# Grouping the bf16 products, pairing the state updates and placing the opening's zero products in an mLSTM plus gated-MLP kernel

## The chip, the cores and the metric

The kernel runs on one core of one Trainium2 chip. A core has five instruction engines: TensorE (PE in the profile, with its weight loads listed as PEld), VectorE (DVE), ScalarE (ACT), GpSimd (POOL) and SyncE (SP), which here issues all DMA transfers. The metric is the device time in microseconds of one execution; several executions of the same kernel are run and their median is given.

## The reference

The first half is a recurrent attention (mLSTM) for 4 batches, 8 heads, 768 steps and head size 40. For each step, with gates f and i in log space and a running maximum m:

```python
m_new = max(f[t] + m, i[t])
C = exp(f[t] + m - m_new) * C + exp(i[t] - m_new) * outer(v[t], k[t])
n = exp(f[t] + m - m_new) * n + exp(i[t] - m_new) * k[t]
y[t] = sigmoid(o_gate[t]) * (C @ q[t]) / max(abs(n @ q[t]), 1)
```

The second half takes y as 3072 tokens of 320 features and computes `((x @ w_a) * (x @ w_b)) @ w_out`, with 1536 hidden features. All inputs and outputs are float32; the weights arrive as float64 bit patterns and are converted on the chip.

## The kernel before

**Attention in chunks.** The 768 steps of each batch are cut into 6 chunks of 128 steps, so there are 24 chunks (chunk n is time piece c = n // 4 of batch b = n % 4). Within a chunk the recurrence is a masked product: pS holds the products of k and q per head, gbc the exponentials of the gates (also the product of both, which becomes the left operand), pV the product with v (42 columns for a head: 40 of v, one of ones for the normalizer, one pad), pI the contribution of the state carried in from earlier chunks, and pU the update of that state, k times the weighted v (vw), 8 heads of 42 columns each. The state of a batch lives in the tile cst; two heads share its 128 partitions, so every pU matmul has 64 output partitions. pX is the transpose of the finished chunk (osig) into the tiles xh and xl, from which the second half starts.

**Precision.** From chunk 6 on (NF32 = 6) the attention works in bf16 pieces: each float32 operand is split into a high, a middle and a low bf16 part. For pV a head then takes 6 matmuls of 42 columns (pb, gbc's middle part and again pb against va, vr, vl), 48 for a chunk; for pS two matmuls of 128 columns a head, 16 for a chunk in two halves of 4 heads; for pI 16 matmuls of 42 columns. The first chunks use plain float32 products instead, which take two passes on PE. The state used by the bf16 chunks is split in the same way (cb, cr), written to DRAM (c_dram) and read back in another layout (cx).

**The gated MLP in blocks.** Tokens go through the MLP in 9 blocks of 2 or 3 chunks (256 or 384 columns). Each of the 12 hidden pieces (ff) has two accumulators pu (for w_a and w_b), 8 matmuls each in float32r with the operands split in high and low parts (xh, xl and the two halves of w), then the product g, its split gh, gl, and 3 matmuls of 320 columns for each chunk into pd.

**Weights.** 32 stages of weights are loaded as raw, converted by ACT and DVE to cw and then to the pair of float32r halves in the tile w (the high half by a cast, the low half by a DVE subtraction).

**What sets the order.** The program is written as Python generators that interleave one attention chunk with the MLP block before it, but no instruction is issued at once. Everything is recorded in a Plan: consecutive matmuls are put together in a node (Plan.add), which is issued as a whole; Plan.cost gives each node an estimated cost; Plan.run goes through time and, for each engine, takes from the ready nodes the one with the smallest rank; Plan.settle repeats this with varied ranks (TURNS turns) and tries each order on TRIALS varied sets of costs; Plan.emit then issues the best order, engine by engine. Some small operations may go to either of two engines (copier: ACT or DVE; adder: DVE or POOL), and the plan chooses. A node of PE holds up to 8 matmuls that write the same accumulator, or (with plan.pair set) different ones. In the opening, while PE has little to do, the plan issues filler matmuls of zeros (warm, 256 columns, line 515 of the profile); ten larger ones (512 columns) come first. Nearly all instructions are issued from line 522, so the profile is read by tile names rather than by lines.

**Buffers and loads near the change.** q and k of chunk n share the tile qk[n % 3], v is in va[n % 3]. The loads of chunk n + 2 are recorded at the start of chunk n (aside, letter L). vr and vl, the lower parts of v, have two buffers each, vw one, cb one. pU is written to the PSUM ring of the attention (pat, two banks) from chunk 6 on.

The functions that the change touches are:

## Time and profile before

| what | value |
|---|---|
| median of 3 runs | 534.64 us (534.57 to 535.79) |
| the profiled execution | 534.12 us |
| its span, first to last instruction | 532.3 us |
| PE busy | 523.2 us, 98% of the span |
| PE weight loads busy | 497.1 us |
| DVE busy | 411.4 us, 77% |
| ACT busy | 236.3 us, 44% |
| POOL busy | 147.9 us, 28% |
| mean granted TensorE clock | 0.994 |

The profile gives start times in microseconds from the first instruction of the span. A matmul's listed duration runs until its result is complete, and matmuls overlap, so what a matmul costs PE is the step from its start to the start of the next one, not its listed duration. A weight load (PEld) overlaps the matmul before it. Where a row covers several matmuls (x2, x16), its time is that of all of them. In a group view the columns after the bar are the total busy time, the mean of one in ns, and the idle time of the engine before these instructions with what ended it.

### The profile page before, as it was taken

What the parts mean: (1) busy time and instruction counts of PE and PEld (TensorE: products, weight loads), DVE (VectorE), ACT (ScalarE), POOL (GpSimd) and SP (SyncE); (2) the same over time, 40 slices, a digit from 0 to 9 for tenths busy, and PEclk for the clock granted to TensorE, in tenths of its full rate; (3) what the DMA queues carried; (4) which work ended last, traced back from release to release, by engine and by line L of the source; (5) the groups of instructions that cost most, each with busy time, mean ns of one, the idle gap of its engine ahead of it and who ended that gap; (6) DMA issues with size and microseconds to landing.
All of it is one profiled execution on the core that took longest, in us unless ns stands there. A gap on an engine that the chain in (4) does not pass through costs nothing.

```text
span 532.3 us, 12505 instructions
## 1 busy us (share of the span) xinstructions
PE 523.2 (98%) x4862; PEld 497.1 (93%) x4862; DVE 411.4 (77%) x919; ACT 236.3 (44%) x568; POOL 147.9 (28%) x194
## 2 busy tenths in 40 slices
PE   8889999999999999999999999999999999999997
PEld 6679999999999999999999999999999999999997
DVE  5999999799979859888599776888489848843332
ACT  5759997543456142346243344543215515212111
POOL 2015134414326505534223423526050301000000
PEclk9899999999999999999999999999999999999999
DMA  9998866978696864886755766765537427000001
GB/s 172 305 245 182 238 167 135 137 148 165 117 188 129 148 146 104 155 158 104 169 105 97 158 119 157 155 99 114 130 73 140 93 41 156 2 1 25 2 1 37
DMA packets 198679, 66.77 MB, mean 125 GB/s; under 512 B 184252, under 2 KB 191900, under 8 KB 198620
## 3 DMA queue, kind: packets, MB, share of 16 engines
q1 hardware_dynamic: 198620, 65.98, 59.6%
q8 instruction: 38, 0.62, 0.5%
q14 instruction: 21, 0.17, 0.1%
HBM read 41.11 MB, written 5.97 MB: 88 GB/s over the span
## 4 chain that ended last, share of the span: by engine, by line
PE 81%; DVE 7%; issue 3%; DMA 2%; ACT 2%; SPq 1%; POOL 0%; ACTq 0%; DVEq 0%; POOLq 0%
PE pu L522 46%; PE pd L522 22%; PE pV L522 4%; PE pS L522 3%; PE pU L522 2%; DVE qks L522 2%; DVE w L522 2%; PE pI L522 2%; SPq L522 1%; PE pX L522 1%; DMA qk<-in_k_dram 1%; DVE cw L522 1%; DMA gbc<-g_dram 1%; DMA c_dram<-cb 1%; DVE osig L522 1%
## 5 line engine op out<-in xcount | busy, mean ns | idle before, releaser
L522 PE MATMUL pu<-xh,w 128*128 128x384 f32 (+1 forms) x1080 | 277.2, 325 | 0.1
L522 PE MATMUL pu<-xl,w 128*128 128x384 f32 (+1 forms) x648 | 203.9, 323 | 0.9 <-DVE xl L522 0.9
L522 PEld LDWEIGHTS pu<-xh,w 128*128 128x128 f32 x1080 | 190.0, 189 | 1.7 <-ACT xh L522 0.6
L522 PE MATMUL pd<-w,gh 128*128 128x320 f32 x576 | 135.1, 315 | 0.3 <-ACT gh L522 0.2
L522 PEld LDWEIGHTS pu<-xl,w 128*128 128x128 f32 x648 | 121.1, 189 | 1.4 <-DVE xl L522 1.2
L522 PEld LDWEIGHTS pd<-w,gh 128*128 128x128 f32 x576 | 97.0, 188 | 1.0 <-ACT gh L522 0.7
L522 DVE TENSOR_TENSOR g<-pu,g 128x384 f32<-128x384 f32 (+1 forms) x108 | 54.6, 506 | 53.4 <-PE pu L522 50.2
L522 ACT COPY g<-pu 128x384 f32<-128x384 f32 (+1 forms) x99 | 43.7, 442 | 113.8 <-PE pu L522 112.6
L522 PE MATMUL pd<-w,gl 128*128 128x320 f32 x288 | 86.6, 310 | 0.1
L522 ACT ACTIVATE gbc<-gbc,gtab 128x128 f32<-128x128 f32 x160 | 52.7, 394 | 3.3 <-POOL gbc L522 3.3
L522 PEld LDWEIGHTS pd<-w,gl 128*128 128x128 f32 x288 | 53.4, 188 | 0.3 <-DVE gl L522 0.3
L522 POOL TENSOR_TENSOR gl<-g,gh 128x384 fp32r<-128x384 f32 (+1 forms) x24 | 26.4, 1102 | 81.4 <-ACT gh L522 46.0
L522 DVE TENSOR_TENSOR gl<-g,gh 128x384 fp32r<-128x384 f32 (+1 forms) x84 | 46.4, 553 | 2.1 <-DVE gh L522 0.5
L522 ACT CAST gh<-g 128x384 fp32r<-128x384 f32 (+1 forms) x44 | 20.5, 465 | 39.9 <-DVE g L522 39.8
L522 DVE TENSOR_TENSOR gbc<-pS,gbc 128x512 f32<-128x512 f32 x48 | 32.6, 681 | 4.7 <-ACT gbc L522 3.7
L522 POOL TENSOR_TENSOR vr<-va 128x336 f32<-128x336 f32 x18 | 14.0, 775 | 79.0 <-PE pV L522 71.1
L522 PE MATMUL pV<-va,gbc 128*128 128x42 bf16 (+1 forms) x240 | 34.5, 221 | 0.0
L522 POOL TENSOR_TENSOR vw<-va,gtab 128x336 f32<-128x336 f32 x20 | 16.2, 808 | 64.9 <-PE pU L522 58.1
L522 PEld LDWEIGHTS <-T 120*128 120x128 bf16 x576 | 25.4, 97 | 7.6 <-issue 5.1
L522 DVE TENSOR_TENSOR gbc<-gbc,pb 128x512 f32<-128x512 f32 x36 | 29.4, 817 | 0.4 <-ACT pb L522 0.3
L522 DVE TENSOR_TENSOR pb<-gbc 128x512 bf16<-128x512 f32 x36 | 29.0, 806 | 0.3
L522 POOL TENSOR_SCALAR_AFFINE_SELECT gbc<-gbc 128x1024 f32<-128x1024 f32 x20 | 25.0, 1248 | 11.7 <-DMA gbc<-g_dram 11.7
(109 smaller groups left out, 768.7 us busy)
## 6 DMA issues: line engine op xcount, KB each, us to landing
gbc<-g_dram SPq DMA_DIRECT2D x20, 512.0 KB
qk<-in_q_dram SPq DMA_DIRECT2D x24, 160.0 KB
qk<-in_k_dram SPq DMA_DIRECT2D x24, 160.0 KB
va<-in_v_dram SPq DMA_DIRECT2D x24, 160.0 KB
osig<-in_o_gate_dram SPq DMA_DIRECT2D x24, 160.0 KB
raw<-in_moe_w_out_dram SPq DMA_DIRECT2D x12, 320.0 KB
out_dram<-o SPq DMA_DIRECT2D x24, 160.0 KB
raw<-in_moe_w_a_dram SPq DMA_DIRECT2D x8, 384.0 KB
```

Of the source, the lines that this page charges most:

```text
L522: f(*[real(x) for x in args], **{k: real(x) for k, x in kw.items()})
```

## The change

The change has these parts:

- **Groups.** A PE node may hold 24 matmuls instead of 8 when the stationary operand of the recorded matmul is a bf16 tile, and 16 when plan.pair is set. The 48 matmuls of pV become two nodes of 24 (one for each half of the heads) instead of six of 8, the 16 of pI one node instead of two; the two nodes of pS stay at 8.
- **Order on PE.** Each PE node has now a head (what its first weight load costs), a tail (its last matmul) and a mode (64 rows, 64 columns or full). When a node with a long head would follow a short matmul, Plan.run looks for another ready node with a short head whose rank is not more than BAND = 15 behind and takes that first. The difference of head and tail, and 0.085 us for a change of mode, are added to the planned time. The assumed cost of a float32r matmul changes too.
- **Search.** TURNS goes from 40 to 100, and the varied costs on which orders are tried are spread less.
- **Two chunks' state at once.** The states of two batches lie in one tile (cst2). stage_u does nothing for even n; for odd n it records 16 pU matmuls, 8 for chunk n - 1 and 8 for chunk n, into one accumulator of 336 columns, then one update of both states on DVE (or one copy on ACT) and one split (cb, cr) of double width. The subtractions of the split may now go to DVE or POOL, and the middle cast to ACT or DVE. put_state and get_state are called for both chunks, so the state of an even chunk is written one chunk later.
- **Loads and buffers.** Since pU of chunk n - 1 reads its k only after chunk n, for odd n >= 3 the load of k of chunk n + 2 (which goes to the same tile) is recorded at the end of stage_u(n), q and v stay where they were. vw has two buffers instead of one, vr and vl one instead of two.
- **Zero products.** The fillers of the opening are placed by what PE has done in the last 3.4 us: they fill a known gap while that use is under 80% (FULL), and up to four are put ahead of a node where it is under 42% (LEAST, FORCED).

```diff
 PSUM = bass.MemoryType.PSUM
-TURNS = 40
+TURNS = 100
 TRIALS = 4
...
 SPELL = 3.4133
+BAND = 15.0
+GAP = 0.1
+FULL = 0.8
+LEAST = 0.42
+FORCED = 4
...
 class Node:
-    __slots__ = ("i", "eng", "alts", "calls", "by", "prev", "next", "table", "acc", "wide", "use", "pair", "least")
+    __slots__ = ("i", "eng", "alts", "calls", "by", "prev", "next", "table", "acc", "wide", "use", "pair", "least", "head", "tail", "mode")
...
         self.table, self.wide, self.use = None, True, 0.0
+        self.head, self.tail, self.mode = None, 0.0, 0
...
         if not (
-            alts[0] == "PE" and node is not None and node.eng == "PE" and len(node.calls) < 8
+            alts[0] == "PE" and node is not None and node.eng == "PE" and len(node.calls) < (24 if getattr(refs[1], "size", 4) == 2 else 16 if self.pair else 8)
             and (node.acc[0][0] == okey or self.pair and node.pair)
...
                 elif "float32r" in f32[0]:
-                    occ = cols / 2400 + 0.0135
+                    occ = cols * 0.000452 + 0.0015
                 else:
...
             by[1] = 0.17
+            node.mode = 1 if refs[1].shape[0] <= 64 else 2 if out.shape[0] <= 64 else 0
+            node.tail = occ
+            if node.head is None:
+                node.head = (0.03 if size[1] == 2 else 0.107) / (2 if node.mode == 2 else 1)
             plain = size[1] == 4 and op == "matmul" and "float32r" not in f32[0]
...
         other = {"DVE": "POOL", "POOL": "DVE"}
-        order, count, filling = [], 0, False
+        order, count, filling, mode, tail, recent = [], 0, False, 0, 1.0, []
...
                     found = i
+            if e == "PE" and found is not None and tail < 0.06 and nodes[found].head > tail + 0.04:
+                like = [
+                    (k, i) for k, i in ready[e]
+                    if not done[i] and k < rank[found] + BAND and nodes[i].head < tail + 0.04
+                ]
+                if like:
+                    back.append((rank[found], found))
+                    found = min(like)[1]
+                    ready[e].remove((rank[found], found))
+                    heapq.heapify(ready[e])
             for z in back:
...
                     filling = False
-                z = free[e] + 0.2
+                z, forced = free[e], 0
                 while filling and fixed is None:
                     w = int((z + phase) / SPELL)
-                    z += 0.107 if used.get(w - 1, 0.0) >= 0.375 * SPELL * 2400 else 0.214
-                    if z > t:
+                    span = 0.107 if used.get(w - 1, 0.0) >= 0.375 * SPELL * 2400 else 0.214
+                    lately = sum(u for at_, u in recent if at_ > z - SPELL)
+                    if z + span < t - GAP and lately < FULL * SPELL * 2400:
+                        pass
+                    elif z > 3.0 and lately < LEAST * SPELL * 2400 and forced < FORCED:
+                        forced += 1
+                    else:
                         break
+                    recent.append((z, 256))
                     used[w] = used.get(w, 0.0) + 256
+                    z += span
                     order.append(None)
+                t = max(t, z)
+                recent.append((t, x.use))
+                del recent[:-60]
+                t += max(0.0, x.head - tail)
+                if x.mode != mode:
+                    t += 0.085
+                    mode = x.mode
+                tail = x.tail
                 w = int((t + phase) / SPELL)
...
         odds = [
-            (rng.uniform(0.98, 1.07, n), 1.0 + 0.025 * j, 0.1 * j, SPELL * j / TRIALS)
+            (rng.uniform(1.0 - 0.005 * j, 1.0 + 0.012 * j, n), 1.0 + 0.01 * j, 0.06 * j, SPELL * j / TRIALS)
             for j in range(TRIALS)
...
-    cst = [wpool.tile([P, HH, DV], F32, name=f"cst{b}") for b in range(B)]
+    cst2 = [wpool.tile([P, 2 * HH, DV], F32, name=f"cst{b}") for b in range(B // 2)]
+    cst = [cst2[b // 2][:, b % 2 * HH:(b % 2 + 1) * HH] for b in range(B)]
     cxp = [[wpool.tile([P, H, DV], BF16, name=f"cx{b}_{w}") for w in range(2)] for b in range(B)]
...
         x = nat(n)[1]
-        vr = apool.tile([P, H, DV], F32, tag="vr", name=f"vr{n}")
-        vl = apool.tile([P, H, DV], BF16, tag="vl", name=f"vl{n}")
+        vr = apool.tile([P, H, DV], F32, tag="vr", name=f"vr{n}", bufs=1)
+        vl = apool.tile([P, H, DV], BF16, tag="vl", name=f"vl{n}", bufs=1)
         s["vb"] = (top(x), top(vr), vl)
...
         if c < NC - 1:
-            vw = apool.tile([P, H, DV], F32, tag="vw", name=f"vw{n}", bufs=1)
+            vw = apool.tile([P, H, DV], F32, tag="vw", name=f"vw{n}", bufs=2)
             nc.gpsimd.tensor_tensor(
...
     def stage_u(n):
+
         c, b = chunks[n]
-        if c == NC - 1:
+        if c == NC - 1 or n % 2 == 0:
             return
-        s = st[n]
         if n < 6:
...
             pU = ps_at.tile([P, 512], F32, tag="pat", name=f"pU{n}")
-        pu = pU[:, 0:HH * DV].rearrange("p (h d) -> p h d", h=HH)
-        for h in range(H):
-            r, _, x = half(h)
-            nc.tensor.matmul(
-                pu[r:r + 64, x], nat(n)[0][:, 1, h, :], s["vw"][:, h], start=True, stop=True
-            )
-        t = cst[b]
+        pu = pU[:, 0:H * DV].rearrange("p (h d) -> p h d", h=H)
+        plan.pair = True
+        for j, m in enumerate((n - 1, n)):
+            for h in range(H):
+                r, _, x = half(h)
+                nc.tensor.matmul(
+                    pu[r:r + 64, j * HH + x], nat(m)[0][:, 1, h, :], st[m]["vw"][:, h],
+                    start=True, stop=True,
+                )
+        plan.pair = False
+        t = cst2[b // 2]
         if c == 0:
...
             nc.vector.tensor_tensor(
-                t, t, dec[:, c - 1, b * HH:(b + 1) * HH].unsqueeze(2).broadcast_to([P, HH, DV]),
+                t, t, dec[:, c - 1, (b - 1) * HH:(b + 1) * HH].unsqueeze(2).broadcast_to([P, H, DV]),
                 op=ALU.mult,
...
         yield
-        if n + B < NF32:
-            return
-        cb = apool.tile([P, 3, HH, DV], BF16, tag="cb", name=f"cb{n}", bufs=1)
-        cr = apool.tile([P, H * DV], F32, tag="tmp", name=f"cr{n}")[:, 0:HH * DV]
-        cr = cr.rearrange("t (h d) -> t h d", h=HH)
-        nc.scalar.copy(cb[:, 2], t)
-        nc.gpsimd.tensor_tensor(cr, t, cb[:, 2], op=ALU.subtract)
-        yield
-        if n < 8:
-            nc.scalar.copy(cb[:, 1], cr)
-        else:
-            nc.vector.tensor_copy(cb[:, 1], cr)
-        nc.gpsimd.tensor_tensor(cb[:, 0], cr, cb[:, 1], op=ALU.subtract)
-        states[n] = cb
-        yield
+        if n + B >= NF32:
+            cb = apool.tile([P, 3, H, DV], BF16, tag="cb", name=f"cb{n}", bufs=1)
+            cr = apool.tile([P, H * DV], F32, tag="tmp", name=f"cr{n}")
+            cr = cr.rearrange("t (h d) -> t h d", h=H)
+            nc.scalar.copy(cb[:, 2], t)
+            nc.adder.tensor_tensor(cr, t, cb[:, 2], op=ALU.subtract)
+            yield
+            nc.copier.copy(cb[:, 1], cr)
+            nc.adder.tensor_tensor(cb[:, 0], cr, cb[:, 1], op=ALU.subtract)
+            states[n - 1], states[n] = cb[:, :, 0:HH], cb[:, :, HH:]
+            yield
+        if n > NS and n + 2 < NCH:
+            load_qk(n + 2, (1,))
...
     def stage_d(n):
-        s = st[n] if n < NS else st.pop(n)
+        s = st[n]
         k_ = block[n]
...
         if o == "L" and n + 2 < NCH and n + 2 > NS + 1:
-            load(n + 2)
+            whole = n % 2 == 0 or chunks[n][0] == NC - 1
+            load_qk(n + 2, (0, 1) if whole else (0,))
+            load_v(n + 2)
         if o == "P":
+            put_state(n - 2)
             put_state(n - 1)
...
         if o == "C":
+            get_state(n - 2)
             get_state(n - 1)
...
         c, b = chunks[n]
-        vw = apool.tile([P, H, DV], F32, tag="vw", name=f"vw{n}", bufs=1)
+        vw = apool.tile([P, H, DV], F32, tag="vw", name=f"vw{n}", bufs=2)
         nc.gpsimd.tensor_tensor(
...
-    idle = apool.tile([P, H * DV], F32, tag="vr", name="idle").bitcast(BF16)[:, 0:512]
+    idle = apool.tile([P, H * DV], F32, tag="vr", name="idle", bufs=1).bitcast(BF16)[:, 0:512]
     nc.vector.memset(idle, 0.0)
...
             if n == 0:
-                load(NS + 1)
+                load_qk(NS + 1, (0,))
+                load_v(NS + 1)
+            else:
+                load_qk(NS + 1, (1,))
         squash(0, NS, B - NS)
...
         yield from attention()
```

The written-out orders of the two programs are compared at three places. The first is on PE, at the state update of chunk 13. In these rows pV13 is the accumulator of chunk 13, pU13 the state update, vw12 and vw13 the weighted v of chunks 12 and 13, and gbc13, pb13, va1, vr13 operands of pV. Before:

```order
L522 MATMUL pV13_4174<-va1_84,gbc13_3624 128x42
L522 MATMUL pU13_4191<-vw13_3910,qk1_81 64x42 x8
L522 LDWEIGHTS gbc13_3624
L522 MATMUL pV13_4174<-vr13_3613,gbc13_3624 128x42
L522 LDWEIGHTS pb13_0_3965
```

The change:

```order
L557 MATMUL pV13_4060<-vr13_3848,gbc13_3479 128x42
L557 LDWEIGHTS pb13_0_3864
L557 MATMUL pV13_4060<-va1_84,pb13_0_3864 128x42
L557 MATMUL pU13_4087<-vw12_3489,qk0_80 64x42 x8
L557 MATMUL pU13_4087<-vw13_3547,qk1_81 64x42 x8
L557 MATMUL pd3_0_3373<-w30_1334,gh3_10_4018 128x320 x2
L557 MATMUL pd3_0_3373<-w30_1334,gl3_10_4023 128x320
```

The update of chunk 12 has moved from its own place to directly ahead of that of chunk 13. In the whole program pU comes in 20 separate places before and in 10 now.

The second place is on PE at the start of chunk 15, whose first product is pS15_0; pu4 and pd4 are accumulators of MLP block 4, T15 the transposed q and k. Before, the two nodes of pS15 stand apart, between float32r matmuls:

```order
L522 MATMUL pS15_0_4594<-T15_0_4406,T15_1_4444 128x128
L522 MATMUL pu4_5_1_4570<-xl4_3485,w12_716 128x384
L522 MATMUL pd4_1_4359<-w13_821,gh4_3_4463 128x320
L522 MATMUL pd4_0_4331<-w13_821,gh4_3_4463 128x320 x2
L522 MATMUL pd4_0_4331<-w13_821,gl4_3_4467 128x320
L522 MATMUL pd4_1_4359<-w13_821,gh4_3_4463 128x320
```

The change:

```order
L557 LDWEIGHTS gbc14_3860
L557 MATMUL pV14_4440<-vr14_4205,gbc14_3860 128x42
L557 LDWEIGHTS pb14_1_4343
L557 MATMUL pV14_4440<-va2_85,pb14_1_4343 128x42
L557 LDWEIGHTS T15_1_4286
L557 MATMUL pS15_0_4491<-T15_0_4318,T15_1_4286 128x128
```

pS15_0 now follows the last of the 48 matmuls of pV14 with no float32r matmul between. Counted over the whole PE order, a bf16 run of the attention is followed by a matmul into pu or pd 99 times before and 44 times now.

The third place is on DVE in the opening, right after the first gates (qks2_88, cx3). pS0 and gbc0 belong to chunk 0, T1 is the transposed q or k of chunk 1, cw, raw0, qks0 and w0 are the first stage of weights. Before:

```order
L522 COPY cx3_1_101<-qks2_88 32x256
L522 TENSOR_TENSOR gbc0_231<-pS0_0_221,gbc0_231 128x4x128
L522 COPY T1_251<-pT1_1_246 128x512
L522 TENSOR_TENSOR gbc0_231<-pS0_1_223,gbc0_231 128x4x128
L522 TENSOR_SCALAR cw_289<-raw0_176 128x384
L522 SCALAR_TENSOR_TENSOR cw_289<-qks0_86,cw_289 128x384
```

The change:

```order
L557 COPY cx3_1_99<-qks2_88 32x256
L557 TENSOR_SCALAR cw_239<-raw0_164 128x384
L557 COPY T1_252<-pT1_0_231 128x512
L557 SCALAR_TENSOR_TENSOR cw_239<-qks0_86,cw_239 128x384
L557 TENSOR_TENSOR gbc0_225<-pS0_0_241,gbc0_225 128x4x128
L557 TENSOR_TENSOR gbc0_225<-pS0_1_243,gbc0_225 128x4x128
```

A copy of T1 and the first two steps of the first weight now stand ahead of the product of pS0 with gbc0. The opening's 256-column zero products are 52 before and 65 now.

## The prediction

> **What bounds the kernel now.** I read the page first (the span and the busy shares), then the busy times by windows, then who PE waits for after the opening.
>
> ```profile
> span 532.3 us, 12505 instructions
> PE 523.2 (98%) x4862; PEld 497.1 (93%) x4862; DVE 411.4 (77%) x919; ACT 236.3 (44%) x568; POOL 147.9 (28%) x194
> ```
>
> ```profile
> core 0: us, PE busy (x) PEld busy (x) DVE busy (x) ACT busy (x) POOL busy (x), PEclk, DMA share, GB/s
> 45.00:80.00 35.00, 34.80 (x324) 33.09 (x322) 33.98 (x82) 34.48 (x84) 10.27 (x14) 1.00 0.75 190
> 100.00:460.00 360.00, 359.55 (x3513) 344.49 (x3512) 295.26 (x643) 147.30 (x366) 118.35 (x135) 1.00 0.64 127
> ```
>
> ```profile
> PE pu L522 <- DVE xl L522: 0.9, 1, 0.9
> PE pE L522 <- ACT gbc L522: 0.5, 1, 0.5
> PE pS L522 <- DVE xl L522: 0.3, 1, 0.3
> PE pd L522 <- ACT gh L522: 0.2, 1, 0.2
> PE pU L522 <- DVE xl L522: 0.2, 1, 0.2
> ```
>
> PE bounds nearly everything: from 100 to 460 us it is busy 359.55 of 360 us, and its waits from 31 us to the end (the third fence is all of them: us in total, times, longest) sum to 2.1 us. DVE has room there (295 of 360), but not from 45 to 80 us, where DVE (33.98 of 35) and ACT (34.48) are as full as PE. So there are two stages. Late, the time is the sum of the steps between PE's matmuls; a change helps by making these steps smaller. Early, until the last weights are converted, vector work sets how soon PE can go on, and the opening before it is a chain through DVE:
>
> ```profile
> 10.24 0.69 DVE L522 TENSOR_TENSOR gbc<-pS,gbc 128x512 f32<-128x512 f32 x1 [3.70 <-ACT gbc L522]
> 30.08 0.56 DVE L522 TENSOR_TENSOR xl<-pX,xh 128x384 fp32r<-128x384 f32 x1
> 30.69 0.39 PE L522 MATMUL pu<-xl,w 128*128 128x256 f32 x1 [0.93 <-DVE xl L522]
> 77.95 1.45 DVE L522 TENSOR_TENSOR w<-cw,w 128x384 fp32r<-128x384 f32 x2
> 79.27 0.57 PE L522 MATMUL pu<-xh,w 128*128 128x256 f32 x2
> 79.67 0.28 PE L522 MATMUL pu<-xl,w 128*128 128x256 f32 x1
> ```
>
> DVE idles 3.70 us until 10.24, then works without a gap; xl for the second chunk comes out at 30.64 and PE starts its dense work at 30.69. At 79.40 DVE ends a low half of w (77.95 + 1.45), and of the two matmuls from 79.27 the second takes until 79.67 - 0.12 = 79.55 to start, instead of 79.39: PE had that weight at the very moment. I take 79.4 us as the point up to which DVE sets the pace.
>
> **Late: what a switch of kind costs.** This is the timeline of PE around chunk 13, the first place of the order above (pU13 is the row at 260.14):
>
> ```profile
> 251.68 0.35 PE L522 MATMUL pu<-xl,w 128*128 128x384 f32 x1
> 251.86 0.34 PE L522 MATMUL pu<-xh,w 128*128 128x384 f32 x1
> ...
> 260.03 0.18 PE L522 MATMUL pV<-va,gbc 128*128 128x42 bf16 x1
> 260.14 0.67 PE L522 MATMUL pU<-vw,qk 128*64 128x42 f32 x16
> 260.74 0.20 PE L522 MATMUL pV<-vr,gbc 128*128 128x42 bf16 x1
> ...
> 261.33 0.18 PE L522 MATMUL pV<-va,gbc 128*128 128x42 bf16 x1
> 261.36 0.42 PE L522 MATMUL pu<-xl,w 128*128 128x384 f32 x1
> 261.62 0.34 PE L522 MATMUL pu<-xh,w 128*128 128x384 f32 x1
> 261.80 0.20 PE L522 MATMUL pV<-vr,gbc 128*128 128x42 bf16 x1
> 261.84 0.21 PE L522 MATMUL pV<-va,pb 128*128 128x42 bf16 x2
> 261.89 0.18 PE L522 MATMUL pV<-vr,pb 128*128 128x42 bf16 x1
> ```
>
> In a row of its own kind a pu matmul of 384 columns steps by 0.18 (251.68, 251.86) and a pV matmul by 0.025 (two from 261.84 to 261.89). The first pu after pV steps by 0.26 (261.36 to 261.62): the way out of bf16 costs 0.085 more. The first pV after pu steps by 0.04 instead of 0.025: the way in costs some 0.02, with a few ns of the pu ahead. So a bf16 run between float32r matmuls costs 0.105 us, whatever its length; this run had 24 matmuls, and the price stood all the same.
>
> The written-out order after the point of 79.4 us (the third use of the same weight) has these ways out to pu or pd: from pV 35 before and 7 in the change, from pS 34 and 17, from pI 26 and 18. That is 53 fewer, 53 x 0.085 = 4.5 us. Ways in from pu or pd fall from 95 to 47, but 20 of the 48 become ways from pV to pS or pS to pI, so I count 28 x 0.02 = 0.5 us. Together 5.0 us.
>
> A visit to pU costs a step of 0.11 from pV (260.03 to 260.14), that is 0.085 too much, and 0.60 from its start to the next pV. The 16 rows (8 heads, two passes) last 0.67 in all and one of them 0.23, from this group row, so 15 inner steps take 0.44 and the last 0.16 instead of 0.03, 0.13 too much. The next pu then steps 0.1 longer, as after the pU group that ends at 38.25:
>
> ```profile
> 38.25 0.38 PE L522 MATMUL pu<-xh,w 128*128 128x256 f32 x1
> 38.47 0.28 PE L522 MATMUL pu<-xl,w 128*128 128x256 f32 x1
> 38.59 0.40 PE L522 MATMUL pu<-xh,w 128*128 128x256 f32 x2
> L522 PE MATMUL pU<-vw,qk 128*64 128x42 f32 x320 | 13.3, 234 | 0.2 <-DVE xl L522 0.2
> ```
>
> (0.22 against 0.12). After 79.4 us there are 15 visits before and 8 in the change: 7 x (0.09 + 0.13) = 1.5, and 11 against 8 ways on to pu or pd, 0.3: 1.8 us. Sum for the late stage: 6.8 us. Bounds: nothing, if the longer groups make PE wait as much as they save, and 6.8 plus the 1 or so of late waits above.
>
> The Trainium skill has a rule that speaks against this: its page "TensorE: Matmul & The Clock Gate", section "Step-by-step: what each phase is for", says that PE's queue pulls weight loads ahead of running matmuls, so that the next weights load while the present matmul runs. By that a change of kind would be free and the late term zero. The trace does not bear it out here, since the step of 0.26 stands behind 24 short matmuls.
>
> **Early: what DVE does less.** In the change, the 3.70 us of idle DVE take three pieces of work that came later (third place of the order): a cw step, a copy of T and a second cw step.
>
> ```profile
> L522 DVE TENSOR_SCALAR cw<-raw 128x384 uint32<-128x384 uint32 x5 | 1.7, 343 | 0.0
> L522 DVE COPY T<-pT 128x512 f32<-128x512 f32 x4 | 2.7, 681 | 0.3 <-PE pT L522 0.3
> L522 DVE SCALAR_TENSOR_TENSOR cw<-qks,cw 128x384 uint32<-128x384 uint32 x20 | 10.8, 559 | 0.2
> ```
>
> 0.34 + 0.68 + 0.56 = 1.6 us, if raw has landed by then. Up to the weight of 79.4 us DVE also copies T twice less (ACT does), 1.4 us; the other exchanges there (fewer casts of w of 320 columns, more of the others, two gl more, one state update less) I take at nothing. So the point comes 3.0 us earlier, at 76.4. Bounds: 0, if ACT, as full as DVE there, is the one that lasts; and 3.0 + 0.5.
>
> **What I cost at nothing.** The 13 more zero products run where PE has no other work:
>
> ```profile
> 24.09 5.24 PE L515 MATMUL warm<-idle 128*128 128x256 bf16 x28
> L522 POOL TENSOR_TENSOR vl<-vr 128x336 bf16<-128x336 f32 x18 | 15.5, 861 | 0.9
> POOL vr L522 <- PE pV L522: 71.1, 7, 19.4
> ```
>
> without that cover 13 x 5.24/28 = 2.4 us. One buffer for vr and vl makes POOL wait for the last pV of a chunk, as it did for 71.1 us already; what is late next is pV of the next chunk, if POOL's two subtractions (0.86 the longer) came too late. On DVE the updates of state are half as many and twice as wide, and more gl falls to it (69 against 57 of 384 columns, for POOL's): some us more on 295 of 360, covered by its idle time. SP issues as many DMAs as before.
>
> **Sum.** Against the profiled execution of 534.12 us: 534.12 - 6.8 - 3.0 = 524.3. The median of the runs stands 0.5 above that execution, so 524.8 us.
>
> **Rivals.**
> *The weights give nothing.* ACT is full with DVE until 80 us; if ACT sets the pace, only 6.8 is left: 534.6 - 6.8 = 527.8. For it: 34.48 of 35 us. Against: what ends last at 79.40 is on DVE.
> *The opening gives more.* In the DVE order xl of the second chunk stands ahead of five scans, and PE could start well before 30.69; if PE fills 3 us more than I count, 521.5. Against: the weight of 79.4 is next to bind.
> *Groups wait.* A node of 24 or 16 holds PE's queue; what stands behind it, all pu and pd, waits with it. The orders have some 40 longer groups; at 0.12 us each 4.8 us go back: 529.6. Against: waits of 2.1 us in all now, for runs up to 48 long.
> *Switches are free in the new order.* If PE loads the next float32r weights while a longer bf16 group still runs, only the 3.0 us of the early stage are won: 531.6. Against: the row at 261.36. The rule of the Trainium skill named above would have it so.
> *Slower: the late load of k.* For 9 odd chunks k can be fetched only after pU of the chunk two before, on SP's queue behind what waits there, such as the transposes:
>
> ```profile
> 97.52 4.38 DMA qk<-in_k_dram
> ```
>
> A load then takes 4.4 us to land, and the split and the transposes follow before pS. It has about one chunk's time, an estimated 20 us (18 chunks in the window from 100 to 460 us), so it should be hidden. It decides from 9.8/9 = 1.1 us of wait on PE for each such chunk; at 1.6 us each the kernel takes 524.8 + 14.4 = 539.2.
>
> **How the numbers follow.** Forecast 0.53, weights give nothing 0.15, opening gives more 0.08, groups wait 0.13, switches free 0.04, late k 0.07. The predicted time is 524.8. Range 520.8 to 530: the low end is the opening's gain in full with the late waits halved, the high end takes in waiting groups; above it lie the last two rivals. A measurement of this kernel can tell 0.3%, 1.6 us, from no change. Faster: all but the late k and a part of the waiting groups (0.05, were they to wait twice as long), 0.88; the same 0.06; slower 0.06.
>
> **What would show it.** PE's busy rows of pU in groups of x32; first steps of 0.26 about half as often; the dense start of PE well before 30.7 us; a third use of the same pu9 weight near 76.4; waits on PE after that not above some 3 us. The forecast is wrong if PE's waits after 31 us exceed 5 us, above all pS behind DMA T, or if the first float32r step after a long bf16 run is longer than 0.26.

## The result and the profile after

The change runs in 526.9 us (median of five executions, 526.72 to 528.93), where the kernel before took 534.64 on the same chip: a ratio of 0.986, 95% interval 0.984 to 0.9881. The forecast was 524.8 with a range of 520.8 to 530, so the time is inside the range and 2.1 us above the forecast. The profiled execution is the slowest of the five (528.93 us, 5.2 below the profiled one of before). The head of its page, and the two windows that were shown of before:

```profile
span 527.1 us, 12448 instructions
PE 513.8 (97%) x4875; PEld 497.0 (94%) x4875; DVE 412.5 (78%) x914; ACT 235.9 (45%) x558; POOL 118.1 (22%) x155
```

```profile
45.00:80.00 35.00, 34.02 (x321) 32.68 (x321) 34.16 (x81) 34.31 (x86) 5.85 (x7) 1.00 0.96 219
100.00:460.00 360.00, 356.52 (x3579) 348.77 (x3578) 298.26 (x654) 145.07 (x352) 96.76 (x106) 1.00 0.64 127
```

PE is busy 9.4 us less than before (523.2), but the span is only 5.2 us shorter: PE now waits. From 100 to 460 us it is busy 356.52 of 360 us (359.55 before). The view of whom PE waits for from 31 us to the end (us in total, times, longest) says where:

```profile
PE pI L557 <- DVE gbc L557: 2.8, 3, 1.9
PE pE L557 <- DVE g L557: 0.8, 1, 0.8
PE pdec L557 <- DVE gtab L557: 0.7, 1, 0.7
PE pU L557 <- DVE xl L557: 0.6, 1, 0.6
PE ptg L557 <- DVE qks L557: 0.5, 1, 0.5
PE pu L557 <- ACT g L557: 0.4, 1, 0.4
PE pu L557 <- DVE w L557: 0.2, 1, 0.2
```

The sum is 6.0 us instead of 2.1, and nearly half of it is a wait that did not exist before: pI for gbc. Of the 6.0 us, 2.6 lie ahead of the third use of the pu9 weight at 79.35 us and 3.4 behind it; before the change it was 1.6 and 0.5. The longest is at 142.98 us. Around it, first PE, then DVE, then POOL:

```profile
142.64 0.34 PE L557 MATMUL pu<-xl,w 128*128 128x384 f32 x1
144.84 0.66 PE L557 MATMUL pI<-cx,T 120*128 120x42 bf16 x16 [1.86 <-DVE gbc L557]
145.34 0.67 PE L557 MATMUL pu<-xl,w 128*128 128x384 f32 x1
145.80 0.84 PE L557 MATMUL pu<-xh,w 128*128 128x384 f32 x2
146.44 0.52 PE L557 MATMUL pu<-xl,w 128*128 128x384 f32 x1
```

```profile
141.82 1.08 DVE L557 TENSOR_TENSOR osig<-osig,den 128x320 f32<-128x320 f32 x1
142.93 1.26 DVE L557 TENSOR_TENSOR osig<-num,osig 128x320 f32<-128x320 f32 x1
144.12 0.68 DVE L557 TENSOR_TENSOR gbc<-pS,gbc 128x512 f32<-128x512 f32 x1
```

```profile
141.50 1.04 POOL L557 TENSOR_TENSOR qks<-r,qks 128x320 bf16<-128x320 f32 x1 [0.53 <-DVE qks L557]
142.51 1.34 POOL L557 TENSOR_SCALAR_AFFINE_SELECT gbc<-gbc 128x1024 f32<-128x1024 f32 x1
```

All 16 matmuls of pI are one node that is issued as a whole; the node goes to the PSUM bank that DVE's product gbc<-pS has still to read, and the pu and pd behind it wait with it. Of DVE's lateness 1.4 us are what two products of osig took, 1.08 and 1.26 us, above their usual 0.48. Behind the wait the pu steps are nearly twice as long (145.80 to 146.44 for two, so 0.32 each instead of 0.174): the granted clock was at half.

The opening, DVE first (the idle time before a row and what ended it are in brackets), then PE:

```profile
8.28 0.36 DVE L557 TENSOR_SCALAR cw<-raw 128x384 uint32<-128x384 uint32 x1 [1.87 <-DMA raw<-in_moe_w_a_dram]
17.11 0.36 DVE L557 TENSOR_SCALAR cw<-raw 128x384 uint32<-128x384 uint32 x1 [1.84 <-DMA raw<-in_moe_w_b_dram]
```

```profile
27.40 0.38 PE L557 MATMUL pu<-xl,w 128*128 128x256 f32 x1 [0.21 <-DVE xl L557]
33.09 0.50 PE L557 MATMUL pu<-xh,w 128*128 128x256 f32 x2 [0.21 <-DVE w L557]
37.80 0.40 PE L557 MATMUL pdec<-ends,sides 32*128 32x64 f32 x2 [0.73 <-DVE gtab L557]
39.98 1.13 PE L557 MATMUL pU<-vw,qk 128*64 128x42 f32 x32
79.23 0.40 PE L557 MATMUL pu<-xh,w 128*128 128x256 f32 x2
```

The 3.70 us in which DVE was idle before have become two waits for raw, 1.87 + 1.84 = 3.71 us. PE's dense start comes earlier, at 27.40 instead of 30.69, and is followed by new waits. pU is in rows of 32, as it should be. The third use of the pu9 weight, the second matmul of the row at 79.23, starts at 79.35. It was to be 76.4; before it stands at 79.45 by its own record (the prediction worked out 79.55 from the rows).

**An account in PE steps.** Every step of an order can be priced at the median step that the same three kinds of matmul in a row take in the trace of before, zero products at nothing; what the trace takes beyond that is lost to waits, zero products and half clock. Before, the steps sum to 506.6 us and 22.1 are lost; in the change 497.9 and 25.7. Cut at the third use of the pu9 weight:

| | steps up to it | lost up to it | steps after it | lost after it |
|---|---|---|---|---|
| before | 60.0 | 19.5 | 446.6 | 2.7 |
| change | 58.8 | 20.5 | 439.1 | 5.2 |

So, before rounding, the late stage gained 7.6 us in steps and gave 2.5 back, and the early stage gained 0.1.

### The profile page after: what moved, and what is told of

It reads as the page before. It is cut to its first block, busy times and chain, and to the rows that moved or that the text cites. A ratio compares the mean times of both kernels' runs of the same rounds, so it can differ in the third digit from the quotient of the medians.

```text
span 527.1 us, 12448 instructions
## 1 busy us (share of the span) xinstructions
PE 513.8 (97%) x4875; PEld 497.0 (94%) x4875; DVE 412.5 (78%) x914; ACT 235.9 (45%) x558; POOL 118.1 (22%) x155
## 4 chain that ended last, share of the span: by engine, by line
PE 82%; DVE 7%; ACT 2%; issue 2%; DMA 1%; SPq 1%; POOL 1%; ACTq 0%; POOLq 0%; DVEq 0%
PE pu L557 46%; PE pd L557 23%; PE pV L557 5%; PE pS L557 3%; DVE qks L557 2%; PE pI L557 2%; PE pU L557 1%; PE pX L557 1%; SPq L557 1%; DMA T<-qks 1%; DVE w L557 1%; DVE cw L557 1%; DVE g L557 1%; DVE osig L557 1%; DVE gbc L557 0%
## 5 line engine op out<-in xcount | busy, mean ns | idle before, releaser
L557 PE MATMUL pu<-xh,w 128*128 128x384 f32 (+1 forms) x1080 | 270.5, 321 | 0.6 <-ACT g L557 0.4
L557 PE MATMUL pd<-w,gh 128*128 128x320 f32 x576 | 133.1, 313 | 0.0
L557 PE MATMUL pd<-w,gl 128*128 128x320 f32 x288 | 87.7, 309 | 0.0
L557 DVE TENSOR_TENSOR gl<-g,gh 128x384 fp32r<-128x384 f32 (+1 forms) x97 | 55.0, 567 | 2.8 <-ACT gh L557 0.6
L557 ACT CAST pb<-gbc 128x512 bf16<-128x512 f32 x27 | 16.7, 619 | 56.4 <-DVE gbc L557 46.5
L557 DVE CAST gh<-g 128x384 fp32r<-128x384 f32 (+1 forms) x75 | 26.8, 357 | 2.2
L557 DVE TENSOR_TENSOR gbc<-gbc,pb 128x512 f32<-128x512 f32 x36 | 27.0, 750 | 0.5 <-ACT pb L557 0.5
L557 DVE TENSOR_TENSOR pb<-gbc 128x512 bf16<-128x512 f32 x36 | 26.9, 747 | 0.3
L557 PEld LDWEIGHTS <-pb 128*128 128x128 bf16 x576 | 23.3, 96 | 2.5 <-issue 1.4
```

The costliest lines, as they stand in the source:

```text
L557: f(*[real(x) for x in args], **{k: real(x) for k, x in kw.items()})
```

## The experiments

The theory after these traces: (A) a way out of a bf16 run costs about 0.1 us whatever the run's length, so the late steps are the gain; (E) the late loss is the kept-together pI, waiting for DVE, and the half clock behind it; (G) in the early stage DVE and its transfers set the pace. The rivals: the gain comes from the longer search (C) or the opening (B); the wait would come out elsewhere (F); ACT (H), or neither (I), sets the early pace. The kernels whose names begin with p keep the order of the change row by row and move or drop only what is named; the others are planned anew. The diffs are shortened to what is altered; those of the p kernels show what is done to the finished order. The runs come from three chips, on which the kernel before took 534.82 us (the parts undone), 534.57 (p_split, p_pI, p_join, p_high) and 535.25 (p_same, p_raw, p_zero, p_best); differences of a few tenths between runs of different chips say little.

### The parts undone

The groups, in Plan.add and Plan.run:

```diff
-len(node.calls) < (24 if getattr(refs[1], "size", 4) == 2 else 16 if self.pair else 8)
+len(node.calls) < (16 if self.pair else 8)
-if e == "PE" and found is not None and tail < 0.06 and ...
+if False and e == "PE" and found is not None and tail < 0.06 and ...
```

> The change, but a PE node again holds at most 8 matmuls (16 where pairing is set), and no node with a short head is preferred; the planned order then has 112 ways out of a bf16 run to pu or pd (the change 44, the kernel before 99) and 10 visits to pU. Theory A (a way out costs 0.085 us and a way in 0.02, whatever the length of the run): the steps of PE alone, priced by the medians of the kernel before, sum to 504.6 us against 497.9, so 526.9 + 6.7 = 533.6 us; since the kept-together pI group can no longer hold PE for DVE's gbc (2.8 us in the change, and the half clock after it some 1.7), up to 4 us less: 529.6 to 533.6. Rival B (ways out cost nothing, the gain is in the opening or the pairing): 526.9 us, within 1.

Measured: 535.65 us, ratio to before 1.0014 (1.0 to 1.0027). Without the groups the change gains nothing, so rival B falls. It is 2 us above the upper end of theory A: the steps are as priced, but as much is lost as in the change (25.4 us), at other places:

```profile
PE pd L557 <- DVE gh L557: 1.5, 2, 1.1
PE pV L557 <- DVE num L557: 0.9, 1, 0.9
PE pu L557 <- DVE g L557: 0.8, 2, 0.7
PE pd L557 <- DVE gl L557: 0.7, 1, 0.7
```

That undoing the groups would save the change's waits was my error: the newly planned order has waits of its own.

The pairing, with stage_u, load and put_state as before:

```diff
-if c == NC - 1 or n % 2 == 0:
+if c == NC - 1:
     return
-for j, m in enumerate((n - 1, n)):
```

> The change, but the state is updated chunk by chunk as before (20 visits to pU instead of 10, 8 matmuls each); all else as in the change, the order is planned anew and has 40 ways out of bf16 (44 in the change). Theory A (a visit costs PE some 0.3 us by its two changes of width): the priced steps sum to 501.2 us against 497.9, so 526.9 + 3.3 = 530.2 us. Rival (the visit is free, since PE would wait for the same inputs anyway): 526.9 us, within 1.

Measured: 531.77 us, 0.9936 (0.9914 to 0.9958), 4.9 above the change. Theory A is right in direction, 1.6 short in size. Up to 3 us of the difference are not the visits: 922 steps from pu to pu of 384 columns took 176.7 ns on average, against 173.3 in the trace of the change (3.1 us in all), for which the edit gives no reason. That stays open.

The search alone, in the kernel before:

```diff
-TURNS = 40
+TURNS = 100
-(rng.uniform(0.98, 1.07, n), 1.0 + 0.025 * j, 0.1 * j, SPELL * j / TRIALS)
+(rng.uniform(1.0 - 0.005 * j, 1.0 + 0.012 * j, n), 1.0 + 0.01 * j, 0.06 * j, SPELL * j / TRIALS)
```

> The kernel before with the change's search alone (100 turns, costs spread less); groups of 8, single state updates, zero products by the old rule. The planned order has 97 ways out of bf16 and 20 visits to pU, 22 zero products in the opening. Theory A (the gain lies in the steps of PE, which need the groups and the pairing): priced steps 505.2 us against 506.6, so 534.6 - 1.4 = 533.2 us, within 1.5. Rival C (a longer search alone finds the better order): 529 us or less.

Measured: 532.53 us, 0.9954 (0.9939 to 0.9969). The search alone brings 2.3 us, a part that the prediction did not count at all; the rest needs the groups and the pairing.

Another seed (`default_rng(8)` for `default_rng(7)`):

> The change with another seed of the search, so another of the orders that the same rules lead to: 43 ways out of bf16, 10 visits to pU, priced steps 497.9 us as in the change. Theory A (the time is the sum of the steps plus waits of PE that are chance of the single order): between 524.5 and 528.5 us; 525.5 or less if the wait of pI for gbc at 143 us with the half clock after it is an accident of this order, which would show as pI waiting under 1 us in all. Rival D (the wait belongs to the kept-together pI, whatever the order): pI waits about 2 to 3 us for gbc again, and 526.9 within 0.5.

Measured: 524.87 us (524.08 to 525.1). pI waits for gbc nowhere, the clock never goes to half between 5 us and the end, and the steps sum to the same 497.9 us. The wait of 1.86 us is an accident of the one order, not what the longer group costs in every order: theory A, not D.

### The price of a way out

In the change's own order the last two matmuls of a pu or pd node are moved into the pV group behind it:

```diff
+new = [(p, p.calls[:-2]), (x, x.calls[:8]), (p, p.calls[-2:-1]),
+       (x, x.calls[8:16]), (p, p.calls[-1:]), (x, x.calls[16:])]
```

> The change's order row by row, except that wherever a pV group of 24 follows a group of pu or pd, the last two matmuls of that group are moved into the pV group, behind its 8th and its 16th matmul (the same matmuls, the same sums, 64 ways out of bf16 instead of 44). Theory A (0.085 out and 0.02 in, whatever the length): 20 x 0.105 = 2.1 us, priced by rows 1.9, so 526.9 + 2.0 = 528.9 us. Rival B (the next float32r weights load behind the bf16 matmuls that still run): 526.9 us, within 0.4.

Measured: 527.42 us (526.8 to 528.22), 0.5 above the change's 526.9: by the medians neither theory. The trace tells why, and settles it. Between the same two pu matmuls, about 148 and 439 us, there are 16 more ways out. Rows of the unaltered order (the run p_same, below), then of p_split:

```profile
148.98 0.68 PE L557 MATMUL pu<-xh,w 128*128 128x384 f32 x3
...
439.26 0.28 PE L557 MATMUL pu<-xl,w 128*128 128x256 f32 x1
```

```profile
147.09 0.68 PE L557 MATMUL pu<-xh,w 128*128 128x384 f32 x3
...
250.94 0.18 PE L557 MATMUL pV<-vr,pb 128*128 128x42 bf16 x1
250.97 0.39 PE L557 MATMUL pd<-w,gh 128*128 128x320 f32 x1
251.20 0.19 PE L557 MATMUL pV<-vl,pb 128*128 128x42 bf16 x1
...
439.01 0.28 PE L557 MATMUL pu<-xl,w 128*128 128x256 f32 x1
```

290.28 us in the one, 291.92 in the other: 1.64 / 16 = 0.103 us for each way out and in, where theory A said 0.105. A single pd between two pieces of pV steps by 0.23 us (250.97 to 251.20) instead of the 0.147 that it takes among its own kind. By the reading of the Trainium skill's rule that the prediction weighed (page "TensorE: Matmul & The Clock Gate", section "Step-by-step: what each phase is for") these 16 would have cost nothing; this run is against that reading. The length of the run does not matter either: in the trace of the change the first pu of 384 columns steps by 0.26 us at full clock behind runs of 16, 24 and 56 bf16 matmuls alike. What hides the price in the whole time of the two traces is the start of the stretch, 147.09 against 148.98: half clock came in the one and not in the other, though both wait there.

### The wait of pI

Each pI node is moved behind up to 1.5 us of the pu and pd that follow it:

```diff
+while k + 1 < len(seq) and passed < 1.5:
+    y = seq[k + 1][0]
+    if y is None or y.tag != "mlp" or x.i in y.prev:
+        break
+    passed += 0.16 * len(y.calls)
+    k += 1
+seq.insert(k, seq.pop(j))
```

> The change's order row by row, except that each pI group of 16 stands behind up to 1.5 us of the pu and pd matmuls that followed it (where none of its own results is needed by them), so that PE works while DVE's gbc is late. Ways out of bf16 rise from 44 to 52, priced steps by 0.5 us. Theory E (the late loss of the change is pI waiting for gbc, 2.8 us, and the half clock of 3.41 us that follows the longest of these waits, some 1.7 us): pI's waits fall under 0.8 us, the clock stays full at 145 us, and 526.9 + 0.5 - 3.5 = 523.9 us (523 to 525.5). Rival F (what DVE is late with comes out at the next group that needs it): 526.9 or more, with other waits of 2 us and over in place of pI's.

Measured: 523.72 us (523.46 to 523.97), 0.9791 (0.9773 to 0.9809): theory E to 0.2 us. The same place, and PE from 100 to 460 us:

```profile
142.77 0.73 PE L557 MATMUL pd<-w,gh 128*128 128x320 f32 x4
143.60 0.56 PE L557 MATMUL pI<-cx,T 120*128 120x42 bf16 x16
144.00 0.42 PE L557 MATMUL pu<-xl,w 128*128 128x384 f32 x1
```

```profile
100.00:460.00 360.00, 359.32 (x3613) 350.76 (x3612) 298.51 (x659) 144.69 (x352) 95.71 (x105) 1.00 0.64 126
```

DVE is as late as before, but PE has work, and the wait comes out nowhere else (rival F): the waits after 31 us are those of the change without pI's. That the median agrees to 0.2 us is in part luck: from the third use of the pu9 weight on p_pI's trace is 4.2 us shorter than that of the change, more than the 3.0 that theory E allows, and 1.0 us came ahead of it, where the move changes nothing.

### When a wait costs half clock

The change's order again, unaltered:

> The change's order, row by row, nothing altered: a second look at the change, on the chip on which the next three run. Theory E (pI's wait for gbc at 143 us and the half clock behind it belong to this order): 526.9 within 1 us, pI waits 2 us or more for gbc, and the clock goes to half after 141 us. If that is an accident of one execution, neither shows, and the time is 525 us or less. The third use of the pu9 weight tells what is the change's and what the execution's: 79.35 in the first trace of the change, 78.3 in the two orders that differ from it only later; I expect 78.3 to 79.4.

Measured: 528.1 us (526.31, 526.69, 528.1, 528.38, 528.54); the profiled execution shows pI waiting 2.6 us and half clock after 145 us, as theory E has it. With the runs in which the same wait was not followed by half clock, the traces agree on what decides, though no run moved the wait against the clock's steps on purpose. The clock records of every run change only at steps of 3.41 us from the first record. The windows below are two such steps each, the one that holds the wait and the next (the second number is PE's busy time, the one before the last two the granted clock). First the change, then p_same, p_split and p_raw (below):

```profile
141.61:145.03 3.42, 1.55 (x16) 1.33 (x16) 3.39 (x5) 0.39 (x2) 2.24 (x2) 1.00 0.78 150
145.03:148.44 3.41, 3.41 (x25) 3.41 (x22) 3.09 (x7) 2.32 (x7) 0.80 (x2) 0.50 0.53 85
```

```profile
141.66:145.08 3.42, 1.70 (x24) 1.47 (x24) 3.35 (x6) 0.97 (x3) 1.40 (x2) 1.00 0.80 153
145.08:148.49 3.41, 3.41 (x14) 3.41 (x14) 3.07 (x7) 2.58 (x8) 1.51 (x2) 0.50 0.95 141
```

```profile
141.05:144.46 3.41, 1.86 (x25) 1.64 (x24) 3.34 (x6) 0.86 (x2) 1.66 (x2) 1.00 0.79 154
144.46:147.88 3.42, 3.42 (x23) 3.42 (x22) 3.42 (x9) 2.42 (x7) 1.37 (x2) 1.00 0.85 133
```

```profile
138.61:142.02 3.41, 2.61 (x25) 2.39 (x23) 3.38 (x5) 0.00 (x0) 3.07 (x3) 1.00 0.58 110
142.02:145.44 3.42, 2.50 (x29) 2.50 (x29) 3.39 (x8) 2.44 (x7) 0.00 (x0) 1.00 0.77 118
```

Where PE was busy 1.55 and 1.70 us of such a step, the next ran at half clock (and so in p_high, below, after 1.69 us); where it was busy 1.86 us, or where the wait fell across two steps (2.61 and 2.50 busy; in p_join 2.51 and 2.71), it did not. Half clock for 3.41 us costs up to 1.7 us, so the same wait costs 1.9 us or 3.6 by where it falls. Where it falls differs between executions: the first clock record stands 4.0 to 5.9 us after the span's start. The first half clock of the opening, after 22 us, goes by the same steps: the step ahead of it was busy 0.82 us in the change and 1.71 in p_pI, where the clock stayed full. Busy time isn't the exact measure, since in the opening 1.57 us was enough once (p_join) and 1.74 (before), 1.83 (p_zero) and 2.12 (s_search) were too little. The mean granted clock, which is on record for every execution, bears out that times differ by such steps: one of them takes 0.003 off it, and in p_same it is 0.997 at 526.31 and 526.69 us, 0.994 at 528.1 and 528.38, 0.990 at 528.54. In the five executions of the change it does not sort the times (526.87 at 0.993, 526.9 at 0.997); where their steps fell is not on record.

### The early stage

DVE relieved of some 14 us of the conversion (p_join); in a second run high(x) is left out in place of join(x), which relieves ACT of as much (p_high):

```diff
 high(x)
 low(x)
-join(x)
```

> The change's order row by row, except that from the sixth stage of weights on DVE does not put the high and low bits of the weights together (27 instructions of some 0.52 us, 14 us of DVE up to 80 us; that part of the conversion is left out, so the weights are not those of the reference). Theory G (DVE sets how soon the early weights are ready): the third use of the pu9 weight moves from 79.3 to 77 us or earlier and the whole time falls by 2.5 to 5 us, to 522 to 524.4. Rival H (ACT sets it): 79.3 within 0.5, 526.9 within 0.7. Rival I (neither, the raw weights' transfers or PE's own work set it): as H, and the same for the run without ACT's part.

> The change's order row by row, except that from the sixth stage of weights on ACT does not form the high half of the weights (27 instructions of some 0.5 us, 13.5 us of ACT up to 80 us; that part of the conversion is left out, so the weights are not those of the reference). Theory G (DVE sets how soon the early weights are ready): 526.9 within 1, the third use of the pu9 weight at 79.3 within 0.7. Rival H (ACT sets it): that use at 77 us or earlier, and 522 to 524.4 us in all. Rival I (transfers or PE's own work): no change with either run.

Measured: without join 524.7 us (524.52 to 525.17), without high 527.94 (526.03 to 528.11). ACT is not what the early stage lasts for: the third use of the pu9 weight is at 78.85 without its work, and at 78.31 (p_split) and 78.35 (p_pI) with it on the same chip. DVE is in part: the use comes before theory G's 77 us, but the time stays above its 524.4. The row that holds that use, in p_same, in p_pI (the same early order) and without join:

```profile
78.72 0.40 PE L557 MATMUL pu<-xh,w 128*128 128x256 f32 x2
```

```profile
78.23 0.40 PE L557 MATMUL pu<-xh,w 128*128 128x256 f32 x2
```

```profile
76.56 0.40 PE L557 MATMUL pu<-xh,w 128*128 128x256 f32 x2
```

By the record of the second matmul of the row, the use comes at 76.67 instead of 78.35 in p_pI, on the same chip, neither with half clock in the opening. Of these 1.7 us all are won by 52 us; from 60 to that use both take 19.2 us. So the part of DVE's conversion that was left out holds PE up only until about 52 us, not until 79.4.

The load of the first o gate behind the second half of the first weights, in SP's queue:

```diff
 DMA raw_237<-in_moe_w_a_dram 64x384
-DMA osig_254<-in_o_gate_dram 128x8x40
 DMA raw_237<-in_moe_w_b_dram 64x384
+DMA osig_254<-in_o_gate_dram 128x8x40
 DMA raw_289<-in_moe_w_b_dram 128x384
```

> The change's order row by row, except that in SP's opening queue the load of the first o gate stands behind the second half of the first weights instead of ahead of it. Theory M (DVE waits for raw, 1.87 us at 8.28 and 1.84 us at 17.11, since the o gate's load is ahead of it, and the dense start of PE follows DVE): the second wait shrinks by about 1 us, the dense start comes 0.5 to 1 us earlier, 0.5 to 1 us less in all. Rival N (the loads share the same transfer rate, so what DVE gains with raw it waits for with the o gate or the next raw): the same time within 0.4 us.

Measured: 525.38 us (524.46 to 526.86), where p_same took 528.1 on the same chip. DVE's second wait for raw, in p_same and in p_raw:

```profile
16.53 0.36 DVE L557 TENSOR_SCALAR cw<-raw 128x384 uint32<-128x384 uint32 x1 [1.23 <-DMA raw<-in_moe_w_b_dram]
```

```profile
15.75 0.36 DVE L557 TENSOR_SCALAR cw<-raw 128x384 uint32<-128x384 uint32 x1 [0.28 <-DMA raw<-in_moe_w_b_dram]
```

The wait shrinks by 0.95 us and the third use of the pu9 weight comes at 77.71 instead of 78.84: theory M. The wait differs between executions, but in no trace of the unaltered early order is it under 0.84 us or the use ahead of 78.31, and the second run with the move (p_best, below) has 77.59. The other 1.6 us of the difference between the medians are not the move's: p_raw's profiled execution has no half clock between 5 us and its end, that of p_same has two steps of it.

The zero products of 256 columns left out:

```diff
+return [z for z in seq if z[0] is not None]
```

> The change's order row by row without any of the 65 zero products of 256 columns (the ten of 512 columns stay). Theory J (they run where PE has no other work and keep the clock up; the opening is a chain through DVE): the time of the order above within 1 us, for PE's own work in the opening runs at half clock for longer, but waits for DVE anyway. Rival K (without them the clock falls at the start of the dense work at 33 us): up to one stretch of 3.4 us at half clock more, so 1.7 us or more above the order above. Rival L (they stand in the way of PE's own work): 1 us or more below it; the row of 28 of them took 5.24 us in the trace of the kernel before.

Measured: 525.71 us (525.11 to 526.01), 2.4 below p_same. The granted clock from 18 to 32 us, without them and with them:

```profile
18.01:31.66 13.65, 7.18 (x31) 6.08 (x32) 13.30 (x30) 6.77 (x18) 0.00 (x0) 0.50 1.06 254
```

```profile
18.01:31.66 13.65, 11.33 (x89) 9.29 (x88) 13.30 (x29) 8.81 (x20) 0.00 (x0) 0.87 1.09 272
```

They do keep the clock up: without them four steps run at half clock. But DVE is as busy in both, and the third use of the pu9 weight comes only 0.66 us later (79.50 against 78.84). That is within the 1.0 us (78.31 to 79.35) by which traces of the unaltered early order differ, and DVE's second wait for raw was 2.40 us there, so it isn't shown that the 0.66 are theirs. So far theory J. That the whole is nevertheless shorter comes from 143 us on: pI waits 1.2 us in all instead of 2.6, none of it at this place, and half clock does not follow. PE comes to this pS 1.0 us later there, DVE to its osig products 0.45 earlier, and these take 0.48 and 0.97 us, 0.9 less than in p_same. The two effects cannot be had apart in this run; rival L has the sign of the total, but not for its reason.

Both moves together, pI later and raw earlier:

> Both moves together: each pI group behind up to 1.5 us of following pu and pd matmuls, and the first o gate's load behind the first weights. The first alone gave 523.72 us. By theory M 522.7 to 523.3; by rival N 523.7 within 0.4.

Measured: 523.45 us (522.99 to 524.12), 0.9777 (0.9752 to 0.9803). It beats both kernels, the change by some 3.5 us (by 4.7 its order on the same chip, p_same). Beside p_pI's 523.72, from another chip, the second move isn't told apart by the medians; in the traces the third use of the pu9 weight comes at 77.59 instead of 78.35.

## Why the prediction was right or wrong

**The bound.** Right for the late stage: PE's steps make the time, and PE is busy 359.32 of 360 us again once pI's wait is gone.

**Late, 6.8 us.** The price of a switch was right (0.103 in p_split for 0.105), whatever the length of the run, and the priced steps after the third use of the pu9 weight fell by 7.6 us. The term's lower bound named what took some of it back, groups that make PE wait; I gave that rival 4.8 us from many small waits, and it was 2.5 us net. The three waits of pI and the half clock behind the longest cost some 4.5 us: by the account above 5.2 us are lost after the third use of the pu9 weight, and without these waits (p_pI) 0.5. "PE waits after that not above some 3 us" nearly held, with 3.4; the step that failed is that a wait was priced at its own length, for the half clock behind one of 1.86 us cost nearly as much again. The waits after 31 us came to 6.0, above the 5 at which I had called the forecast wrong; 2.6 of them are those of the opening. Pairing (4.9 us when undone, 3.3 of it in priced steps) was undersized at 1.8, with the reserve made above, and the search's 2.3 us had no term.

**Early, 3.0 us.** This term failed. The measured gain up to the third use of the pu9 weight is 0.1 us in the first trace of the change, 0.6 to 1.1 in those of p_same and of the two orders that differ only later. The condition that I wrote down without pricing, "if raw has landed by then", is where: raw had not landed, and DVE waits 3.71 us for it. The second error is the point of 79.4 us: a weight that is ready just when PE takes it is not proof that DVE sets the pace up to there. By p_join, DVE sets it until about 52 us.

**At nothing.** The single buffer of vr and vl and the late load of k stood: no row of PE's waits names pV behind POOL or pS behind a transfer. The zero products, all 65 of them, cost nothing that can be told from PE's time in the opening.

**The rivals.** "The weights give nothing" had the nearest time (527.8 for 526.9), but its reason, ACT, is refuted by p_high. "Groups wait" had the right mechanism. "The opening gives more" had the earlier dense start (27.40 us), but in that trace only 0.1 us of it was left at the third use of the pu9 weight (its 521.5 is a slip: 3 us below 524.8 is 521.8). "Switches are free" fell with p_split, the slower rival with the waits.

**The sum.** 534.12 - 7.6 + 2.5 - 0.1 = 528.9, the profiled execution; the median of the change lies 2 us under it, the median of before 0.5 above its own. That the time lies in the range is in part luck: nearly all of the early 3.0 us was missing, and the range had its room above for waiting groups, not for that.

## What to carry to other kernels

Where PE is the bound, a long group of short matmuls saves a fixed price for every run that it does away with (0.1 us here for the way in and the way out together), but it holds up all of PE's queue when its first input is late: put it where its input is ready with room to spare, behind other ready work. Before an engine's idle time is counted as room for work, look up when that work's data lands. And price a wait on PE with the clock behind it: one that leaves PE less than about half busy in one step of the clock costs nearly twice its length.

## What the runs showed that I had not expected

**The clock goes by fixed steps.** The wait of pI, 1.5 to 1.9 us, was followed by 3.41 us of half clock in the change, p_same and p_high, and not in p_split, p_join and p_raw; what differed was how much of it fell into one step (1.55 to 1.70 us busy against 1.86 and more). The Trainium skill, page "TensorE: Matmul & The Clock Gate", section "Part 1: The HAM clock gate (the "warmup" mystery)", says that activity is watched in a free-running window of 3413 ns; these records agree. It gives one idle window as the condition of half clock, and here a window in which PE was busy for 45 to 50% of its length was enough.

**DVE beside POOL.** The products of osig on DVE, both inputs in SBUF, over the whole profile of the change (ns, shortest, median, longest):

```profile
L557 DVE TENSOR_TENSOR osig<-osig,den x21: 476/485/1372, 18.1 to 457.8; 128x320 f32<-128x320 f32 x21
L557 DVE TENSOR_TENSOR osig<-num,osig x20: 474/484/1426, 92.5 to 458.3; 128x320 f32<-128x320 f32 x20
```

None of them that ran while POOL was idle took more than 0.50 us; of the twelve that overlapped an instruction of POOL seven took 0.75 to 1.43. The two before the wait of pI were such: 1.08 + 1.26 instead of 2 x 0.48 made DVE 1.4 us late. The Trainium skill, page "GPSIMD Engine Reference", section "8. Key points", says that GpSimd shares its SBUF interfaces with VectorE and that instructions with two SBUF inputs contend; the trace agrees. No run here took POOL's work away, so that it alone made DVE late isn't shown.
